# Kernel: gated linear attention and a mixture of experts. The first six units' steps in a written-out order, k times r made to wait for the port, the gate's weights loaded earlier

## The chip, the cores and the metric

One core of one Trainium2 chip. The metric is the device time of one execution of the program in microseconds, as a median over runs. A core has five engines that run on their own and wait for each other by semaphores: TensorE (PE; its weight loads are shown as PEld), VectorE (DVE), ScalarE (ACT), GpSimd (POOL) and SyncE (SP), which here issues nearly all DMA transfers. Each engine takes its instructions strictly in the order in which they were written.

## The reference

All numbers are float32. First a gated linear attention over 4 batches, 8 heads, 768 tokens and a head size of 48, then a mixture of 8 experts of which each token uses one (3072 tokens of 384 values, hidden size 1024):

```python
f = 1.0 / (1.0 + np.exp(-f_logit))
for t in range(S):
    state = f[:, :, t, :, None] * state + np.einsum('bhd,bhe->bhde', k[:, :, t], v[:, :, t])
    y[:, :, t] = np.einsum('bhd,bhde->bhe', q[:, :, t], state)
x = y.transpose(0, 2, 1, 3).reshape(B * S, H * D)
logits = x @ w_gate
expert_idx = np.argmax(logits, axis=1)
# softmax value of the chosen expert is gate_w
y[rows of e] = np.maximum(x[rows of e] @ w1[e], 0.0) @ w2[e]
out = gate_w[:, None] * y
```

## The kernel before

The attention part is cut into 12 units (`NU`). A unit is a chunk of 128 tokens of two batches with all heads; its q, k and f come as tiles of 128 x 8 x 128 (512 KB each), its v as 384 KB. Units 0 and 1 hold the first chunk of the two pairs of batches, 2 and 3 the second chunk, and so on: each unit needs the state of the unit two before it. A unit goes through these steps, each a small function:

- `load`: SP issues the transfers. q has 4 buffers, k 3, f 2, v 3, so that a load waits until the unit that used the buffer is done with it. Hardware DMA transfers also take turns on eight completion semaphores.
- `steps` and `log` (ACT): exp of -f and ln(1 + that), which is minus the logarithm of the forget gate, in g. `total` (DVE): the running sum of it over the chunk, a scan. `growth` (ACT): r = exp(sum). `decay` (ACT): exp(-sum).
- `by_r`: k times r, on DVE for unit 0 and on POOL for all others. `by_decay` (DVE): q times decay. `ends` and `last_decay` (POOL): small copies of the last column.
- `score` (PE): k times q in two halves, `mask` (DVE): four masked copies out of PSUM, `within` (PE): masked scores times v into `yt`.
- `keys` (PE): k transposed into `kp`, `keep` (ACT): copied to `kn`, `added` (PE): kn times v into `dp`, `update` (DVE, then POOL): the new state, the sum of old state and dp, times the last decay. `before` (PE): q times the old state, added to `yt`.
- `settle` (ACT): yt copied to `ys`. `rows` (PE): ys turned to token rows and multiplied with the gate's weights, into `xp`; the weights lie in a tile of constants, `fpack`. `lay` (ACT): the rows copied to `xr`. `Route` (DVE, mostly small instructions): the chosen expert, the place of each token's row in its expert's region, the gate's value; then POOL scatters the rows to DRAM.

The schedule is written by hand (`manual_schedule`): each engine runs its instructions in the order of the calls. Before, units 0 and 1 and part of 2 and 3 are written out call by call ahead of a loop `for n in range(1, NU + 2)`, and the loop has special cases for n of 1, 2 and 3. In an iteration the loop does the scores, keys and dp of unit n, steps of units n + 1 to n + 3 ahead, and rows and routing of unit n - 2. `warm(24)` and `warm(12)` are matmuls of zeros on `pad` that TensorE runs while it has nothing to do.

The constants come in two parts: `load_first_consts` issues the mask and the identity from ACT's queue, `load_consts` the rest from SP's, after q of unit 3. `load_gate` issues four small transfers of the gate's weights into the same tile as the rest of the constants, behind f of unit 5; they wait until the constants have landed.

In `by_r` a k times r on POOL waits for an instruction on DVE, if one stands in the list `routed`:

```python
if routed:
    tc.add_manual_dep(ins, routed.pop().name, SYNC, reason="the port of both")
```

Before, only the loop puts instructions there (the last of `choose` or of `fill`), so k times r of units 1 to 4 waits for its own operands alone.

After the attention part, experts' weights (`w1t`, `w2t`, 1536 KB each) and the scattered rows are loaded, and two wide matrix products per expert run on TensorE (`widen`, `narrow`). The change leaves this part as it is.

Of the kernel before, what the change touches and what calls it, by code (L numbers as in the profile page):

```python
# [118 lines left out]
def _bc(ap, axis, n):  # L119
    shape = list(ap.shape)  # L120
    shape.insert(axis, n)
    return ap[tuple([slice(None)] * axis + [None])].to_broadcast(shape)
# [3 lines left out]
def kernel(  # L126
# [41 lines left out]
    def load_first_consts():  # L168
        nc.scalar.dma_start(mpack, nc.inline_tensor(mv, name="c_mpack").ap())
        nc.scalar.dma_start(ident, fdram[:, slice(*fat["ident"])])  # L170
# [249 lines left out]

    with ExitStack() as st:
# [25 lines left out]
        routed = []  # L447
        SYNC = mybir.DependencyInfo(mybir.DependencyClass.Sync, mybir.DependencyReason.DATA)
# [8 lines left out]
        def load(u, names, parts=(slice(None),)):  # L457
            x = units[u]
            for n in names:
                src = {"q": qu, "k": ku, "f": fu, "v": vu}[n]  # L460
                if n == "v":
                    x[n] = ld.tile([128, 2, H, D], F32, name=n, bufs=3)
                else:
                    x[n] = held[n][u % len(held[n])]
                for part in parts:
                    nc.sync.dma_start(x[n][:, part], src[u][:, part])
# [19 lines left out]
        def total(u, part=whole):  # L486

            x = units[u]
            if "sum" not in x:
                x["sum"] = wk.tile([128, SEG, CR], F32, name="sum")  # L490
            nc.vector.tensor_tensor_scan(  # L491
                x["sum"][:, part].rearrange("p s c -> p (s c)"),
                x["g"][:, part].rearrange("p s c -> p (s c)"),
                cap[:, part].rearrange("p s c -> p (s c)"),
                0.0,
                OP.add,
                OP.min,
            )
# [25 lines left out]
        def last_decay(u):  # L524
            x = units[u]
            x["last"] = wk.tile([128, SEG], F32, name="last", bufs=3)
            nc.gpsimd.tensor_copy(x["last"], x["dec"][:, :, C - 1])  # L527

        def by_decay(u, part=whole):
            x = units[u]  # L530
            q = x["q"][:, part]
            nc.vector.tensor_tensor(q, q, x["dec"][:, part], op=OP.mult)
# [32 lines left out]
        def within(u, a):  # L565

            x = units[u]
            if a == 0:
                x["yt"] = yt
            for p, h, _ in heads():  # L570
                nc.tensor.matmul(  # L571
                    x["yt"][DP * (h ^ a) : DP * (h ^ a) + D, a, p],
                    lhsT=x["v"][:, a, 2 * p + h],
                    rhs=x["at"][:, a, h, p],
                    start=p == 0,
                    stop=x["old"] is None,
                    skip_group_check=True,
                )
# [38 lines left out]
        def update(u):  # L617

            x = units[u]
            new = wk.tile([128, SEG, D], F32, name="state", bufs=4)  # L620
            last = _bc(x["last"], 2, D)
            if x["old"] is None:
                nc.vector.tensor_copy(new, x["dp"])
            else:
                nc.vector.tensor_tensor(new, x["dp"], x["old"], op=OP.add)
            states[u % 2] = new
            return lambda: nc.gpsimd.tensor_tensor(new, new, last, op=OP.mult)
# [70 lines left out]
        load(0, "f", ab)  # L698
        load(0, "kq")
        load(1, "f")  # L700
        load_first_consts()
        load(1, "kq")
        for i in (1, 0):
            nc.gpsimd.memset(scores[i], 0.0)
        def warm(count):

            for _ in range(count):
                nc.tensor.matmul(yt[:, 0, 0], lhsT=pad[:, 0:C], rhs=pad[:, 0:C], start=True, stop=True)

        warm(24)  # L710
        for part in ab:
            steps(0, part)
            total(0, part)
        load(2, "f")
        load(0, "v")
        for part in ab:
            growth(0, part)
            by_r(0, part, nc.vector)
            decay(0, part)
            by_decay(0, part)  # L720
        ends(0)
        last_decay(0)
        for part in ab:
            steps(1, part)
        load(3, "f")
        load(2, "k")
        load(1, "v")
        load(2, "q")
        load(3, "q")
# [44 lines left out]
        score(0, 0)  # L774
        score(0, 1)
        keys(0)
        warm(12)
        for part in ab:
            total(1, part)
        for a in range(2):  # L780
            for h in range(2):
                mask(0, a, h)
        for part in ab:
            growth(1, part)
            by_r(1, part)
        for part in ab:
            decay(1, part)
            by_decay(1, part)
        ends(1)
        last_decay(1)  # L790
        steps(2)
        total(2)
        keep(0)
        steps(3, logs=False)
        growth(2)
        load_consts()
        load(3, "k")
        load(4, "f")
        load(2, "v")
        load(5, "f")  # L800
        load_gate()

        for n in range(1, NU + 2):
# [3 lines left out]
            rt = None  # L807
            if here < NU:
                units[here]["old"] = states[here % 2]
            if 2 <= last:  # L810
                settle(last)
            if later and later[0] < NU - 1:
                later[1].weigh()
# [3 lines left out]
            if ahead and n != 2:  # L817
                by_r(n + 1)
                ends(n + 1)
# [7 lines left out]
            if n == 1:  # L827
                units[0]["old"] = None
                added(0)
                update(0)()  # L830
            if ahead and not 1 < n < 4:
                decay(n + 1)
                last_decay(n + 1)
# [3 lines left out]
            if n == 2:  # L837
                growth(n + 1)
                by_r(n + 1)
                ends(n + 1)  # L840
            if 1 < n < 4:
                decay(n + 1)
                last_decay(n + 1)
# [4 lines left out]
            if n == 1:  # L848
                log(3)
                within(0, 0)  # L850
                within(0, 1)
                settle(0)
# [6 lines left out]
            if 2 < n < NU - 2:  # L859
                total(n + 2)  # L860
            if n == NU - 2:
                by_decay(n + 1)
            first_half = 1 < n < NU - 2
            if first_half:
                within(back, 0)
            if 0 <= last:
                rt = rows(last, later[1] if later else None)
                lay(last)
# [6 lines left out]
            if n == 2:  # L875
                total(n + 2)
# [13 lines left out]
            if n == 2:  # L890
                settle(1)
            if n + 2 < NU and n != 1:
                growth(n + 2)
# [7 lines left out]
            if n == 1:  # L901
                total(3)
# [15 lines left out]
            if n == 1:  # L918
                load(n + 3, "q")
# [4 lines left out]
            if 1 < n and n + 3 < NU:  # L924
                load(n + 3, "q")
            if n + 5 < NU:
                load(n + 5, "f")
            if n == 1:
                load_first_pads()
# [398 lines left out]
```

## Time and profile before

| | |
|---|---|
| median of 14 runs | 400.96 us (399.82 to 403.68) |
| profiled execution | 400.77 us, span 398.9 us, mean granted TensorE clock 0.983 |
| TensorE busy | 382.2 us of the span (96%) |
| DVE, ACT, POOL busy | 170.3, 103.1, 116.7 us |
| DMA | 95.04 MB, mean 238 GB/s |
| DMA from 5 to 25 us | 383 to 411 GB/s |
| span of the attention part | 0 to about 121 us |

The span is from the first to the last instruction; the profiled execution's own time is 1.9 us longer. Busy times say how long an engine ran, not whether the end waited for it. The timeline merges equal instructions and gives, in brackets, how long the engine was idle before and which instruction released it. Each fp32 matmul of the program appears as two instructions in the trace. Line numbers (L543) are those of the kernel before.

### The profile page before, as it was taken

Reading aid. Unit: us, or ns where it says so; the run is one execution under the profiler, and the core shown is the slowest. Engines: PE = TensorE matmul, PEld = TensorE weight load, DVE = VectorE, ACT = ScalarE, POOL = GpSimd, SP = SyncE. Lnnn points to the kernel's source line nnn. Section 1 sums busy time; section 2 is a strip of 40 time slices with the busy share of each in tenths; the row PEclk is TensorE's granted clock in tenths of the full one; section 3 lists DMA queues with packets and bytes.
Section 4 is the critical chain, followed back from the end, with each engine's and each line's share of the span. In section 5 each row is a group of like instructions: output and inputs, shape, how many; then the busy total and the mean of one; then the engine's idle time right before and its main releaser. Section 6 shows DMA issues by size and latency. Waiting matters only on the chain.

```text
span 398.9 us, 7727 instructions
## 1 busy us (share of the span) xinstructions
PE 382.2 (96%) x3062; PEld 269.1 (67%) x3062; DVE 170.3 (43%) x365; ACT 103.1 (26%) x190; POOL 116.7 (29%) x118
## 2 busy tenths in 40 slices
PE   7898999999997999999999999999999999999993
PEld 7877898999986787777555555664556556555462
DVE  6899988989661452212112113113712113111360
ACT  6888877774431100000010010010000000001000
POOL 5378868797607220010100100100100100100011
PEclk9999999999998699999999999999999999999998
DMA  8999657679954157959339899989145349994141
GB/s 287 391 332 361 235 204 258 231 223 330 399 164 156 50 165 221 306 137 302 103 117 361 228 379 393 282 341 340 39 154 196 99 144 394 397 413 154 26 175 41
DMA packets 51515, 95.04 MB, mean 238 GB/s; under 512 B 20824, under 2 KB 40731, under 8 KB 49424
## 3 DMA queue, kind: packets, MB, share of 16 engines
q1 hardware_dynamic: 48016, 84.76, 62.6%
q0 software_dynamic: 3168, 9.64, 6.4%
q8 instruction: 25, 0.41, 0.4%
q10 hardware_dynamic: 288, 0.08, 0.2%
q14 instruction: 18, 0.15, 0.1%
HBM read 79.46 MB, written 15.21 MB: 237 GB/s over the span
## 4 chain that ended last, share of the span: by engine, by line
PE 86%; DMA 4%; DVE 3%; ACT 2%; issue 1%; another core or an unknown queue 1%; SPq 0%; POOL 0%; POOLq 0%; DVEq 0%; ACTq 0%
PE hps L316 27%; PE yps L332 23%; PE yps L1107 7%; PE xp L663 5%; DMA f<-in_fu_dram 4%; PE yt L571 4%; PE s L543 4%; PE s L316 3%; PE hps L1081 3%; PE yp L332 3%; PE yt L592 3%; PE dp L608 2%; PE kp L558 2%; DVE sum L491 1%
## 5 line engine op out<-in xcount | busy, mean ns | idle before, releaser
L316 PE MATMUL hps<-xT,w1t 128*128 128x352 f32 (+2 forms) x384 | 110.1, 447 | 0.0
L316 PEld LDWEIGHTS hps<-xT,w1t 128*128 128x128 f32 x384 | 72.7, 190 | 37.2 <-issue 1.9
L332 PE MATMUL yps<-w2t,hT 128*128 128x384 f32 x288 | 94.4, 487 | 0.0
L189 POOL DMA_INDIRECT out_dram<-ysb,dst x24 | 23.3, 969 | 224.5 <-DVE ysb L343 216.1
L332 PEld LDWEIGHTS yps<-w2t,hT 128*128 128x128 f32 x288 | 54.6, 190 | 38.6 <-issue 1.5
L326 ACT ACTIVATE hT<-hps 128x352 f32<-128x352 f32 (+2 forms) x28 | 13.7, 491 | 200.7 <-PE hps L316 190.6
L328 DVE TENSOR_SCALAR hT<-hps 128x352 f32<-128x352 f32 (+2 forms) x28 | 15.6, 558 | 93.0 <-PE hps L316 93.0
L343 DVE TENSOR_SCALAR ysb<-yps,tg 128x384 f32<-128x384 f32 x22 | 13.6, 618 | 74.4 <-PE yps L332 55.7
L189 POOL DMA_INDIRECT xs<-xr,posi x24 | 33.1, 1381 | 25.4 <-DVE ex L222 12.7
L549 DVE COPY_PREDICATED at<-mpack,s 128x512 f32<-128x512 uint8 x48 | 31.1, 730 | 6.2 <-PE s L543 6.2
L509 POOL TENSOR_TENSOR k<-k,r 128x1024 f32<-128x1024 f32 (+1 forms) x12 | 26.5, 2213 | 19.9 <-ACT r L505 10.5
L491 DVE TENSOR_TENSOR_SCAN sum<-g,cap 128x1032 f32<-128x1032 f32 (+1 forms) x14 | 28.9, 2061 | 3.1 <-ACT g L484 3.0
L663 PE MATMUL xp<-fpack,ys 128*128 128x104 f32 x192 | 26.0, 285 | 2.1 <-ACT ys L633 1.4
L1107 PE MATMUL yps<-qw,hqT 128*32 128x192 f32 (+1 forms) x192 | 26.9, 381 | 0.0
L543 PE MATMUL s<-q,k 64*128 64x128 f32 x384 | 24.7, 278 | 2.0 <-POOL last L527 1.4
L663 PEld LDWEIGHTS xp<-fpack,ys 128*128 128x128 f32 x192 | 23.2, 194 | 4.4 <-issue 1.8
L571 PE MATMUL yt<-at,v 128*48 128x128 f32 x384 | 25.1, 277 | 0.0
L543 PEld LDWEIGHTS s<-q,k 64*128 64x128 f32 x384 | 22.4, 188 | 3.9 <-POOL last L527 1.6
L571 PEld LDWEIGHTS yt<-at,v 128*48 128x48 f32 x384 | 20.0, 123 | 2.6 <-issue 1.5
L1107 PE MATMUL yps<-w2t,hT 128*32 128x384 f32 x192 | 21.4, 487 | 0.0
L316 PE MATMUL s<-xT,w1t 128*128 128x128 f32 x96 | 15.5, 316 | 2.0 <-issue 1.9
L633 ACT COPY ys<-yt 128x512 f32<-128x512 f32 x24 | 12.9, 592 | 16.2 <-PE yt L592 11.6
(114 smaller groups left out, 366.3 us busy)
## 6 DMA issues: line engine op xcount, KB each, us to landing
qw<-in_moe_w_dram SPq DMA_DIRECT2D x16, 1536.0 KB
w1t<-in_moe_w_dram SPq DMA_DIRECT2D x8, 1536.0 KB
w2t<-in_moe_w_dram SPq DMA_DIRECT2D x8, 1536.0 KB
k<-in_ku_dram SPq DMA_DIRECT2D x12, 512.0 KB
q<-in_qu_dram SPq DMA_DIRECT2D x12, 512.0 KB
f<-in_fu_dram SPq DMA_DIRECT2D x11, 512.0 KB
xs<-pad SPq DMA_DIRECT2D x8, 600.0 KB
v<-in_vu_dram SPq DMA_DIRECT2D x12, 384.0 KB
```

Source lines behind the costliest of these rows:

```text
L189: ins = nc.gpsimd.indirect_dma_start(out=dst, out_offset=bass.IndirectOffsetOnAxis(ap=idx, axis=0), in_=src, in_offset=None, bounds_check= ...
L316: nc.tensor.matmul(x["h"][:, f], lhsT=w[0][:, j, b * 128 : b * 128 + 128], rhs=x["xT"][:, j], start=j == 0, stop=j == KD - 1,)
L326: nc.scalar.activation(to, x["h"], AF.Relu)
L328: nc.vector.tensor_scalar(to, x["h"], 0.0, None, op0=OP.max)
L332: nc.tensor.matmul(yp, lhsT=x["hT"][:, f, t * C : t * C + C], rhs=w[1][:, f, :], start=f == 0, stop=f == NF - 1,)
L491: nc.vector.tensor_tensor_scan(x["sum"][:, part].rearrange("p s c -> p (s c)"), x["g"][:, part].rearrange("p s c -> p (s c)"), cap[:, part ...
L509: ins = on.tensor_tensor(k, k, units[u]["r"][:, part], op=OP.mult).ins
L543: nc.tensor.matmul(ps[h][:, p], lhsT=x["k"][r, s], rhs=x["q"][r, s], start=True, stop=True)
L549: nc.vector.copy_predicated(x["at"][:, a, h], _bc(causal, 1, HP), x["ps", a][h])
L571: nc.tensor.matmul(x["yt"][DP * (h ^ a) : DP * (h ^ a) + D, a, p], lhsT=x["v"][:, a, 2 * p + h], rhs=x["at"][:, a, h, p], start=p == 0, st ...
L663: nc.tensor.matmul(xp[:, p], lhsT=x["ys"][:, a, p], rhs=wx[:, p, 0:XW] if a else wx[:, p, E:WX], start=True, stop=True,)
L1107: nc.tensor.matmul(yp[r], lhsT=h[:, f, at : at + T], rhs=w[:, f, cols], start=f == 0, stop=f == NF - 1, skip_group_check=True,)
```

## The change

The calls ahead of the loop and the loop's iterations 1 to 5 give way to a table, `FIRST_STEPS`. Each word is a piece of work, a unit and sometimes a half; a loop over the table calls the piece. The loop proper now starts at n = 6. The sets of transfers and of computing steps stay; their order on each engine changes:

- PE: 17 and 4 zero matmuls instead of 24 and 12; the keys of a unit ahead of its scores; in units 1, 2, 4 and 5 the two halves of the scores apart; `within` of units 0 and 1 much earlier (that of unit 0 before the keys of unit 1).
- DVE, ACT and POOL: the masks of a unit, the copies, scans and exponentials stand in a new order through unit 8.
- SP: the first constants, which ACT issued, are issued by SP in front of q of unit 0. The other constants stand behind q of unit 2, and the gate's four transfers right behind them, in front of f of unit 4, k of unit 3, v of unit 2 and q of unit 3.
- k times r on POOL in units 1 to 6 waits for the DVE scan or q times decay that was written last before it (`port["latest"]`).
- `last` has four buffers instead of three.

```diff
 def load_first_consts():
-    nc.scalar.dma_start(mpack, ...)
-    nc.scalar.dma_start(ident, ...)
+    nc.sync.dma_start(mpack, ...)
+    nc.sync.dma_start(ident, ...)
...
+    FIRST_STEPS = """
+        lf0a lk0 consts0 lq0 lf1 lk1 lq1 fill17 exp0a ln0a scan0a exp0b lf2 lv0 ln0b r0a
+        scan0b dec0a r0b dec0b exp1a byr0a ln1a byd0a byr0b byd0b scan1a exp1b lf3 lk2 lv1
+        lq2 consts1 gate0 kp0 ln1b r1a scan1b sc0a keep0 mask0a r1b sc0b dec1a mask0b byr1a
+        byr1b dp0 fill4 ends0 exp2 lf4 lk3 lv2 lq3 upd0 byd1a wi0a wi0b ln2 kp1 sc1a dec1b
+        keep1 set0 scan2 last1 dp1 last0 ends1 byd1b r2 exp3 lf5 dec2 sc1b lq4 lk4 lv3 ln3
+        mask1a wi1a mask1b byr2 upd1 wi1b byd2 kp2 sc2b scan3 keep2 xp0 ends3 mask2b exp4
+        lf6 pads0 upd0p r3 byr3 lay0 sc2a lk5 lv4 lq5 ends2 dp2 set1 mask2a ln4 wi2b dec3
+        last2 upd2 scan4 wi2a kp3 keep3 bef2 dec4 last3 byd3 byd4 r4 xp1 sc3a exp5 lf7 byr4
+        lay1 upd1p ends4 set2 ln5 sc3b lk6 lv5 lq6 oh1 dp3 mask3a mask3b exp6 lf8 sc4a upd3
+        ln6 last4 kp4 scan5 mask4a wi3a ends5 keep4 r5 wi3b dec5 scan6 wgh1 xp2 bef3 lay2
+        sc4b lk7 lv6 lq7 set3 dec6 place1 exp7 lf9 upd2p dp4 ln7 wi4a mask4b wi4b upd4 byr5
+        byd5 kp5 upd3p scan7 byd6 keep5 bef4 last6 last5 exp8 lf10 xp3 oh3 sc5a mask5a r6
+        sc5b lk8 lv7 lq8 ends6 lay3 dp5 byr6 wgh3 mask5b ln8 r7 set4 upd5 upd4p send5
+    """
...
+    def do_by_r(u, part):
+        routed[:] = [port["latest"]] if u else []
+        by_r(u, piece(part), nc.gpsimd if u else nc.vector)
...
+    for what, u, part in re.findall(r"([a-z]+)(\d+)([abp]?)", FIRST_STEPS):
+        DO[what](int(u), part)
...
-    for n in range(1, NU + 2):
+    for n in range(FIRST, NU + 2):
```

In the table, l stands for a load (lf4: f of unit 4), sc for `score`, kp for `keys`, wi for `within`, dp for `added`, bef for `before`, xp for `rows`, oh, place and wgh for the routing, fill for the zero matmuls.

## The prediction

> **What bounds the kernel now.** I read the page first, then TensorE's timeline of the first 46 us, the busy times by stage, the waits before 42.2 us, and the order of the built instructions, which shows what the table moves.
>
> From the page:
>
> ```profile
> PE 382.2 (96%) x3062; PEld 269.1 (67%) x3062; DVE 170.3 (43%) x365; ACT 103.1 (26%) x190; POOL 116.7 (29%) x118
> PE 86%; DMA 4%; DVE 3%; ACT 2%; issue 1%; another core or an unknown queue 1%; SPq 0%; POOL 0%; POOLq 0%; DVEq 0%; ACTq 0%
> ```
>
> TensorE is the bound, and the 4% of DMA stands at the front. Busy times by stage (stretch and length, then busy us of PE, PEld, DVE, ACT, POOL; granted clock; DMA share; GB/s):
>
> ```profile
> 0.00:42.18 42.18, 35.70 (x457) 32.89 (x457) 36.66 (x47) 34.74 (x59) 27.35 (x27) 1.00 0.91 334
> 42.18:114.00 71.82, 71.82 (x1214) 65.27 (x1216) 59.85 (x139) 47.77 (x88) 51.88 (x50) 1.00 0.79 274
> 126.00:136.00 10.00, 8.00 (x32) 6.72 (x31) 1.75 (x11) 1.62 (x5) 4.66 (x9) 0.50 0.27 105
> ```
>
> From 42.18 to 114 us TensorE has no idle time at all: there the change can bring nothing, and whatever the front saves arrives whole at 114 us and, if the later steps are merely shifted, at the end. So the question is how much TensorE loses before 42.18. Its timeline (start, us, then idle before in brackets):
>
> ```profile
> 9.64 2.06 PE L543 MATMUL s<-q,k 64*128 64x128 f32 x32
> 11.62 1.09 PE L558 MATMUL kp<-fpack,k 128*128 128x128 f32 x8
> 12.55 2.84 PE L708 MATMUL yt<-pad 128*128 128x128 f32 x24
> 16.81 2.06 PE L543 MATMUL s<-q,k 64*128 64x128 f32 x32 [1.42 <-POOL last L527]
> ...
> 24.62 2.06 PE L543 MATMUL s<-q,k 64*128 64x128 f32 x32 [0.57 <-POOL rend L515]
> ...
> 29.07 2.00 PE L663 MATMUL xp<-fpack,ys 128*128 128x104 f32 x16 [0.35 <-ACT kn L563]
> ...
> 33.51 1.14 PE L608 MATMUL dp<-v,kn 128*64 128x48 f32 x32 [1.43 <-ACT xr L693]
> ...
> 42.18 1.14 PE L608 MATMUL dp<-v,kn 128*64 128x48 f32 x32 [0.54 <-ACT xr L693]
> ```
>
> After unit 0's scores and transposed keys (12.55), TensorE loses 2.84 of filler and 1.42 + 0.57 + 0.35 + 1.43 + 0.54 of idle: 7.15 us. This is all that reordering can win after 12.55. What else the front waits for:
>
> ```profile
> POOL k L509 <- ACT r L505: 10.5, 4, 4.4
> ACT g L476 <- DMA f<-in_fu_dram: 3.6, 3, 1.8
> ```
>
> **The sum of the new order.** I walk TensorE's new sequence with the old rows' durations; per unit s 1.99, kp 1.02, dp 0.92, yt of a unit's own chunk 1.9, yt from the state 1.02, xp 1.96; DVE's scan 2.31, four masks 2.57, q times decay 1.28; ACT 0.53 for half a tile, 0.96 for a whole one; k times r on POOL 2.37.
>
> Start. The constants leave ACT's queue and stand on SP's ahead of q of unit 0. ACT's two issues (0.4 each) lay beside its table load of 1.28, and SP's two more are hidden, since the queue's transfers of 1.3 each run behind its issues of 0.45: nothing either way. The first filler, 17 for 24, ends near 8, before the first k is ready. The bytes ahead of unit 1's f are the same, and ACT's start on unit 1 (9.62, released by f) stays. k·r of unit 0 ends at 9.71 on DVE; kp's second half 0.5 and s 1.99 end at 12.2 instead of 12.55. That is lost again, because dp comes next and needs v of unit 0.
>
> v of unit 0. Ahead of its end stand seven tiles of 512 KB, 384 KB of v and 80 KB of constants, 4.14 MB. The DMA moved 0.88 MB by 5 us and 2.01 more by 10; the other 1.25 at 396 GB/s end at 13.2. For f of unit 1 the same count gives 8.2, and ACT was released at 9.6, 1.4 later; so v is there at about 14.5. From 12.55: 1.95 idle. The filler of 4 costs 4/12 of 2.84, 0.95.
>
> Unit 1. yt of unit 0 starts at 16.3 (masks end 13.55 + 2.57 = 16.1, covered). kp, s, dp, s of unit 1 follow unbroken until 22.3. The last two masks then end about 23.5 where TensorE wants them at 23.2: 0.3.
>
> Unit 2. ACT does kn, ys and r from 19.0 and is done at 22.2; k·r on POOL ends at 24.55, and q times decay on DVE at 25.8: TensorE waits 0.1 and 0.2.
>
> The gate's weights. SP meets them right behind the constants they overwrite, and holds f of unit 4, k of 3, v of 2 and q of 3 behind that wait. The constants land at about 21.9 (before they landed one 1.3 us tile later, by 23.2, where SP's wait of 3.4 us for them ended). Four issues take 1.79 and f's own 0.4: 24.2. The first half tile of f took 2.7 from issue to ACT's start, a whole tile 0.65 more: f at 27.5, k at 28.8, v at 29.8, q at 31.1, since the queue has run empty in between. Before, ACT started on that f at 25.86. Then exp 1.15, r 0.96, three copies 0.8 and ys 1.06 end at 31.5; yt of unit 2 wants that at 30.95. k has 0.9 to spare (k·r starts at 29.7), q 3.6, v nothing. TensorE waits 0.25 for dp and 0.55 for yt. Bounds: nothing if f lands a microsecond sooner, 2 us if it and v are 1.2 later, as tails in this trace can be (8.2 against 9.6); I take 0.8.
>
> Units 3 to 5. kp of 4 waits 0.3 for DVE's state; yt of 4 waits 1.0, since its second pair of masks stands behind the scan of unit 6 and the nine small routing steps (0.22 each); s of 5 waits 0.3 and dp of 5 0.3.
>
> The port wait. k·r of unit 5 waits for the scan of unit 6, to 47.9 though r is ready at 45.4. It ends at 50.3, and its transposes come at 53: covered by 2.7; without that cover up to 2.4. Where both engines meet today, POOL already stands still: its copies of 128x8 take 0.19 alone and 2.2 beside a scan. A gain is bounded by what DVE loses to POOL, a scan of 2.62 for 2.31, 0.3 a unit. I take nothing. The behind-queue of each k·r (end copies, state times decay, scatters) has unit-long slack. The fourth buffer of last has no instruction.
>
> Lost after 12.55: 1.95 + 0.95 + 0.3 + 0.3 + 0.8 + 0.3 + 1.0 + 0.3 + 0.3 = 6.2. The same walk through the old order loses 8.0 where the trace shows 7.15, so it overstates waits; scaled by 0.89 the new order loses 5.5. Gain 7.15 - 5.5 = 1.6.
>
> **Rivals.** First, slower: the clock. There are 1.95 to 2.3 us of idle before dp of unit 0, with 4 fillers instead of 12. Against it: 1.42 and 1.43 us of idle left the clock at 1.00. For it: at 125.8 it fell to half for 10.2 us, and in the 3.4 us before TensorE's longest gap was 1.22, its idle time 1.6 in all. If one gap of about 2 us does that, the next 10.2 us, holding 9 us of work, lose up to 5.1, of which the waits of units 1 and 2 and of the gate absorb 1.4 to 2: 3.1 net, 402.3. It decides where more than about half of some 3.4 us is idle.
>
> By the Trainium skill, "TensorE: Matmul & The Clock Gate", Part 1, the clock halves after at least one idle window of about 3.4 us, free-running; a gap of 2.3 would not do, and the sum would stay 399.2. The row at 125.8 fell with less idle than that, so the measurement decides, and I keep this rival.
>
> Second, faster: the late waits aren't there. Of the 6.2, only 1.95, 0.95 and 0.3 for the first masks are forced by rows; the others are small differences between engines that overlap. Without them the loss is 3.2, the gain 3.95: 396.8.
>
> Third, no change: the hole that SP's wait makes costs its upper bound, or v of unit 0 is 1.2 later; the walk then loses as much as the old order: 400.6 and about what it was. For it: the DMA share of 0.91 over the front leaves no reserve.
>
> **How the numbers follow.** The profiled execution took 400.77 (span 398.9 and 1.9 around it), 0.05% under the median of 400.96. 400.77 - 1.6 = 399.2, for which I give 0.4 (its own range 398.2 to 400.0); the clock 0.2 (402.3), the late waits gone 0.2 (396.8), no change 0.2 (400.6). The range from 396.8 to 402.4 takes in the centres of all. About 0.3%, 1.2 us, is what a measurement of this kernel can tell from no change. Faster by more: most of the first case and the second, 0.54; within it: the third and the edges, 0.25; slower: 0.21.
>
> **What would show it.** In the new profile: dp of unit 0 at about 14.5 after 2 us of idle; SP's wait for the constants ending near 22; ACT starting on f of unit 4 near 27.5; the transposed keys of unit 3 near 33.5 (36.56 before, with an equal amount of work behind it); no idle worth a microsecond after 60; the clock at 1.00 until 114. Wrong if the clock dips before 40, if the DMA share in 20 to 26 stays full, or if the stage after 42 shows new waits that add up to the gain.

## The result: 1.4 to 1.8% slower

On the chip of the first comparison the changed kernel takes 407.48 us (median of 10 runs, 403.59 to 409.23), the kernel before 401.38: ratio 1.0136, 95% interval 1.0111 to 1.016. In a later comparison, on a chip where both are faster, it took 397.49 against 390.24: 1.0182, 1.014 to 1.0224. The forecast was 399.2 and a gain. The profiled execution took 409.48 us (span 407.4, clock 0.974).

The page of the changed kernel, the lines that answer to those of before (busy times, and the chain that ended last by engine):

```profile
PE 384.1 (94%) x3032; PEld 268.8 (66%) x3032; DVE 174.6 (43%) x365; ACT 102.6 (25%) x190; POOL 107.1 (26%) x118
PE 84%; DVE 5%; DMA 3%; another core or an unknown queue 3%; ACT 2%; SPq 1%; issue 1%; POOL 0%; POOLq 0%; ACTq 0%
```

TensorE is busy for about as long as before (384.1 us for 382.2) and the span is 8.5 us longer; DVE's share of the chain has gone from 3 to 5%. The busy times by stage say where (columns as before):

```profile
0.00:42.05 42.05, 35.48 (x490) 32.17 (x490) 33.44 (x45) 33.25 (x59) 20.95 (x25) 1.00 0.82 298
42.05:115.00 72.95, 68.92 (x1059) 61.74 (x1060) 63.33 (x128) 47.33 (x84) 48.63 (x52) 0.95 0.74 264
45.00:48.30 3.30, 3.30 (x22) 2.74 (x20) 3.30 (x4) 1.34 (x3) 0.23 (x2) 0.50 1.02 405
```

The stage after 42 us, in which TensorE had no idle time at all, now has 4.0 us of it, and a clock of 0.95: it is at half from 44.94 to 48.35 (third row) and from 68.83 to 72.25. TensorE's waits of more than 0.5 us from 12 to 116 us, from its timeline (two of 0.19 us stand at 24.59 and 57.45):

```profile
14.76 1.14 PE L625 MATMUL dp<-v,kn 128*64 128x48 f32 x32 [2.16 <-ACT r L523]
32.08 1.14 PE L625 MATMUL dp<-v,kn 128*64 128x48 f32 x32 [1.25 <-DMA v<-in_vu_dram]
43.67 1.94 PE L561 MATMUL s<-q,k 64*128 64x128 f32 x16 [1.61 <-DVE at L567]
56.84 0.42 PE L588 MATMUL yt<-at,v 128*48 128x128 f32 x2 [0.55 <-DVE at L567]
67.06 3.82 PE L561 MATMUL s<-q,k 64*128 64x128 f32 x32 [1.48 <-DVE at L567]
```

The last three wait for masks (L567) of units 3, 4 and 5. The front did gain, but half of what was forecast: the keys of unit 3, with about the same work behind them, start at 34.92 instead of 36.56, 1.6 us ahead, where the forecast had 33.5, 3.1 ahead. And at the state's part of y of unit 6, an equal point for both orders, the changed kernel is 6.6 us behind (86.8 against 80.2). The other 1.9 us of the 8.5 come behind that point; in the transition to the experts this profile has one wait of 3.69 us (at 138.1), which the later profile of the same kernel on another chip doesn't have.

Why the masks are late stands in the timeline of POOL and DVE of the changed kernel (some lines left out):

```profile
39.13 2.36 POOL L527 TENSOR_TENSOR k<-k,r 128x1024 f32<-128x1024 f32 x1 [2.81 <-DVE lg L689]
39.26 0.19 DVE L215 TENSOR_REDUCE mx<-lg 128x4 f32<-128x32 f32 x1
39.48 2.06 DVE L216 TENSOR_TENSOR eq<-lg,mx 128x32 f32<-128x32 f32 x1
...
41.45 0.83 POOL L643 TENSOR_TENSOR state<-state,last 128x384 f32<-128x384 f32 x1
...
41.58 0.75 DVE L217 TENSOR_TENSOR eq<-eq,fpack 128x32 f32<-128x32 f32 x1
...
42.80 2.56 DVE L567 COPY_PREDICATED at<-mpack,s 128x512 f32<-128x512 uint8 x4
```

and the same steps in the kernel before (its lines are numbered one lower here):

```profile
37.00 2.37 POOL L509 TENSOR_TENSOR k<-k,r 128x1024 f32<-128x1024 f32 x1 [1.04 <-ACT r L505]
...
43.52 0.19 DVE L215 TENSOR_TENSOR eq<-lg,mx 128x32 f32<-128x32 f32 x1
43.75 0.19 DVE L216 TENSOR_TENSOR eq<-eq,fpack 128x32 f32<-128x32 f32 x1
...
44.72 2.37 POOL L509 TENSOR_TENSOR k<-k,r 128x1024 f32<-128x1024 f32 x1 [1.28 <-DVE ex L222]
```

Two routing steps of 0.19 us each take 2.06 and 0.75. The first ends when k times r of unit 4 ends on POOL (41.49), the second when the product of state and last decay, which stands right behind it there (L643), ends at 42.28. All masks of unit 3 stand behind the two. Before, k times r of unit 4 (37.00) ran ahead of this choice and had no wait, and that of unit 5 (44.72) waited for the end of the choice (`ex`). In the new order each k times r comes one routing step earlier: that of unit 4 beside the choice, that of unit 5 beside the placing, for whose end k times r of unit 6 waited before. And nothing keeps them apart, since the change put the latest scan or q times decay in the place of the old wait. In unit 5 `counts` (L234) takes 1.70 us for 0.17, in unit 6 the two steps take 1.93 and 0.75.

The Trainium skill, "SBUF — State Buffer", section on its two separate sides, says that VectorE and GpSimd share one port pair as an exclusive lock, and that an operation of VectorE with two SBUF inputs (or in a two-port mode) is shut out while a GpSimd operation that reads SBUF holds it. That agrees with the 2.06 us: L216 has two SBUF inputs and ends when k times r does. L215, with one, took its usual 0.19 us beside the same k times r. The copy L234 also has one, from SBUF to SBUF, and was shut out; whether it runs in such a mode no run here shows.

### The profile page after: what moved, and what is told of

It is laid out like the page before. It is cut to its first block, busy times and chain, and to the rows that moved or that the text cites. A ratio compares the mean times of both kernels' runs of the same rounds, so it can differ in the third digit from the quotient of the medians.

```text
span 407.4 us, 7637 instructions
## 1 busy us (share of the span) xinstructions
PE 384.1 (94%) x3032; PEld 268.8 (66%) x3032; DVE 174.6 (43%) x365; ACT 102.6 (25%) x190; POOL 107.1 (26%) x118
## 4 chain that ended last, share of the span: by engine, by line
PE 84%; DVE 5%; DMA 3%; another core or an unknown queue 3%; ACT 2%; SPq 1%; issue 1%; POOL 0%; POOLq 0%; ACTq 0%
PE hps L317 27%; PE yps L333 23%; PE yps L1114 7%; PE yt L588 5%; PE xp L681 5%; PE s L561 3%; PE yp L333 3%; PE hps L1088 3%; PE yt L609 2%; PE kp L576 2%; PE s L317 2%; DMA f<-in_fu_dram 2%; PE dp L625 1%; DMA v<-in_vu_dram 1%; DVE at L567 1%
## 5 line engine op out<-in xcount | busy, mean ns | idle before, releaser
L190 POOL DMA_INDIRECT xs<-xr,posi x24 | 31.9, 1329 | 25.4 <-DVE counts L234 13.4
L567 DVE COPY_PREDICATED at<-mpack,s 128x512 f32<-128x512 uint8 x48 | 31.3, 725 | 5.6 <-PE s L561 5.5
L561 PE MATMUL s<-q,k 64*128 64x128 f32 x384 | 27.8, 287 | 3.3 <-DVE at L567 3.1
L509 DVE TENSOR_TENSOR_SCAN sum<-g,cap 128x1032 f32<-128x1032 f32 (+1 forms) x14 | 27.9, 1992 | 2.9 <-ACT g L502 2.6
L561 PEld LDWEIGHTS s<-q,k 64*128 64x128 f32 x384 | 24.2, 193 | 6.0 <-issue 4.7
L317 PE MATMUL s<-xT,w1t 128*128 128x128 f32 x96 | 14.0, 291 | 2.7 <-issue 2.6
L1114 PEld LDWEIGHTS yps<-w2t,hT 128*32 128x32 f32 x192 | 7.6, 110 | 13.0 <-issue 12.5
```

Of the source, the lines that this page charges most:

```text
L190: ins = nc.gpsimd.indirect_dma_start(out=dst, out_offset=bass.IndirectOffsetOnAxis(ap=idx, axis=0), in_=src, in_offset=None, bounds_check= ...
L317: nc.tensor.matmul(x["h"][:, f], lhsT=w[0][:, j, b * 128 : b * 128 + 128], rhs=x["xT"][:, j], start=j == 0, stop=j == KD - 1,)
L509: port["latest"] = nc.vector.tensor_tensor_scan(x["sum"][:, part].rearrange("p s c -> p (s c)"), x["g"][:, part].rearrange("p s c -> p (s ...
L561: nc.tensor.matmul(ps[h][:, p], lhsT=x["k"][r, s], rhs=x["q"][r, s], start=True, stop=True)
L567: nc.vector.copy_predicated(x["at"][:, a, h], _bc(causal, 1, HP), x["ps", a][h])
L1114: nc.tensor.matmul(yp[r], lhsT=h[:, f, at : at + T], rhs=w[:, f, cols], start=f == 0, stop=f == NF - 1, skip_group_check=True,)
```

## Experiments

Each ratio is against the kernel before in the same comparison on the same chip (389.95 to 390.24 us in all but the last two runs).

**The changed kernel again.**

> The changed kernel itself once more, beside the four below on one chip, where the kernel before took 390.07 us in the first four runs. On the chip of the first comparison the ratio was 1.0136 and its profile had two spells of half clock of 3.41 us that the kernel before lacked. Theory (collisions of k times r with the routing, 1.61 + .55 + .19 + 1.48 us of idle TensorE, and the two spells that follow them, about 3.4 us together): some 6.5 us over the kernel before here too, ratio 1.015 to 1.019. Rival (the loss is in the transition after 140 us, whose wait was 2 us longer in that one profile): ratio about 1.011, without the spells near 45 and 69.

397.49 us, ratio 1.0182 (1.014 to 1.0224). Its trace has the waits of 2.12, 1.61, 1.41 and 1.48 us again and two spells of half clock, one at 16.6, behind the first gap, and one at 67.8. There is no wait in the transition after 126 us on this chip (TensorE 25.93 of 26 us busy), so that was not the cause.

**The routing behind the masks.** `oh1`, `place1` and `oh3`/`wgh3` are moved in the table so that no masks stand behind them.

```diff
-lq6 oh1 dp3 mask3a mask3b exp6 lf8 sc4a upd3 ln6
+lq6 dp3 mask3a mask3b exp6 lf8 sc4a upd3 oh1 ln6
-dec6 place1 exp7 lf9 upd2p dp4 ln7 wi4a mask4b wi4b
+dec6 exp7 lf9 upd2p dp4 ln7 wi4a mask4b place1 wi4b
-xp3 oh3 sc5a ... byr6 wgh3 mask5b ln8 r7 set4 upd5 upd4p
+xp3 sc5a ... byr6 mask5b ln8 r7 set4 upd5 oh3 wgh3 upd4p
```

> The changed kernel with three words of its table moved: the choices of units 1 and 3 (oh1, oh3) and the placing of unit 1 (place1) stand on DVE behind the masks that they stood in front of; nothing else is touched. Theory A (collision): in the changed kernel k times r runs on POOL beside DVE's small two-input steps of the routing, which then take 2.06 and 0.75 us instead of 0.19 each, and the masks and scores behind them come late; this costs the two idle stretches of 1.6 and 1.5 us and the two 3.4 us spells of half clock that follow them. It expects unit 4's keys at 43 (45.5 in the changed kernel), unit 6's at 64.5 (70.8), no half clock between 40 and 75, and 401 to 403 us instead of 407.5. Theory B (the gate's place on SP alone is what costs): same as the changed kernel within 1 us. Theory C (the table's order as such, many small waits): keys of unit 6 not earlier than 69.

394.53 us, ratio 1.0108 (1.007 to 1.0146). The three waits for masks (1.61, 0.74 and 1.48 us) are gone, and in their stretch TensorE waits 0.29, 0.59 and 0.38 us for other things; the keys of unit 6 start at 63.8 instead of 70.8. But a new wait of 1.98 us comes before the state product of unit 6, followed by 6.83 us at half clock. It is the same kind of meeting, one step on:

```profile
65.19 2.39 POOL L527 TENSOR_TENSOR k<-k,r 128x1024 f32<-128x1024 f32 x1
...
66.03 4.63 DVE L509 TENSOR_TENSOR_SCAN sum<-g,cap 128x1032 f32<-128x1032 f32 x1
...
71.31 1.16 PE L625 MATMUL dp<-v,kn 128*64 128x48 f32 x32 [1.98 <-ACT xr L711]
```

A scan of 2.30 us takes 4.63 beside k times r of unit 7 (to 67.58) and the product of the state behind it on POOL (67.65 to 68.49). The gate's sums stand behind the scan and start at 70.59 us, and what waits for them holds TensorE.

**The gate's weights behind q of unit 3**, instead of ahead of f of unit 4: `gate0` moved behind `lq3` in the table.

> The changed kernel with one word of its table moved: the gate's four transfers stand behind f of unit 4, k of 3, v of 2 and q of 3 on SP instead of in front of them. Theory B (hole in the queue): the DMA share in 20 to 25 us, 0.12 in the changed kernel, is about full, dp of unit 2 no longer waits 1.25 us for v, unit 3's keys come at 33.5 to 34 (34.9), and the whole is 1 to 1.5 us faster if this reaches the end. Theory A (collision decides): the front is earlier, but the collision of k times r of unit 4 with the routing stays, so that about 1 us or less is left at the end: 406.5 to 407.5.

395.96 us, ratio 1.015 (1.0133 to 1.0167). The wait of 1.25 us before the state product of unit 2 is gone; half clock at 14.86 and 45.58 us is mixed into the time, so the gate's place was priced again without it (below).

**The old order with the gate's weights early.** In the kernel before, `load_consts()` and `load_gate()` are moved up, behind q of unit 2 and in front of q of unit 3.

> The kernel before with one step of the change alone: the larger part of the constants and the gate's transfers are issued behind q of unit 2, in front of q of 3, k of 3, f of 4 and v of 2. Theory B: SP holds these loads behind its wait for the constants; f of unit 4 comes some 3 us later than before (ACT took it at 25.9), unit 3's keys at 39 to 41 instead of 36.6, and the whole takes 403 to 405. Theory A: the old order has slack there; at most 1 us slower than before.

397.2 us, ratio 1.0176 (1.015 to 1.0201). The loads stand behind the queue's wait (DMA share 0.09 from 20 to 25 us): TensorE stands idle for 6.29 us at 28.65, and half clock follows for 6.83 us. In the old order this part of the change alone, with the half clock that it sets off, costs as much as the whole change, more than either theory gave it.

**The old order with the new wait.** In the kernel before, k times r from unit 5 on waits for the latest scan or q times decay.

```diff
+if u > 4:
+    routed[:] = [port["latest"]]
```

> The kernel before with one step of the change alone, carried through all later units: from unit 5 on, k times r on POOL waits for the DVE scan or q times decay written last before it, and no longer for the last step of the choice or of the placing. Theory A (collision): k times r of 2.4 us runs beside the routing's small steps on DVE, one or two of which take some 2 us instead of 0.19 in every unit from 5 to 11; DVE has about 1 us to spare per unit, so TensorE is no longer without idle time from 42 to 114; 5 to 10 us slower than before. Theory C: no such stretching, within 1 us of before.

394.75 us, ratio 1.0123 (1.0106 to 1.014), with no spell of half clock before 389 us. One routing step in each unit takes about 2 us beside k times r (the first two lines have it for unit 5), VectorE is busy 69.8 of the 72 us from 42 to 114, and TensorE waits in every unit (last line: what waited for what, us in all, times, longest):

```profile
43.31 2.36 POOL L510 TENSOR_TENSOR k<-k,r 128x1024 f32<-128x1024 f32 x1 [0.18 <-ACT r L506]
43.44 2.28 DVE L216 TENSOR_TENSOR eq<-eq,fpack 128x32 f32<-128x32 f32 x1
...
PE dp L611 <- ACT xr L696: 2.9, 7, 0.6
```

So trading the old wait for the new one costs over 1% by itself, in the old order too.

**The old wait in the new order.** k times r of units 4 to 6 waits for the choice or placing before it again (`byr4` behind `oh1`, `port["latest"]` also set by the routing).

> The changed kernel with one rule of the kernel before: k times r of units 4 to 6 waits for the last step of the routing's choice or placing before it (k times r of unit 4 stands behind the choice in program order), not for the latest scan or q times decay. Theory (the lost wait lets k times r run beside the choice, 2.06 us for a step of .19): L216 and L217 take .19 us each, the masks of units 3 and 5 start 2.4 us earlier, the gaps of 1.61 and 1.48 us and the two spells behind them go, and the time falls by 4 to 6.5 us, to within 2 us of the kernel before. Rival (the order itself, not the wait, makes the collision): k times r only meets the next short steps or the masks, gaps of 1 us or more stay at other places, and the time falls by under 2 us.

395.79 us, ratio 1.0126 (1.0102 to 1.0151): 1.7 us less than the changed kernel, where 4 to 6.5 was expected.

```profile
40.23 0.19 DVE L216 TENSOR_TENSOR eq<-lg,mx 128x32 f32<-128x32 f32 x1
...
41.43 2.37 POOL L527 TENSOR_TENSOR k<-k,r 128x1024 f32<-128x1024 f32 x1 [1.60 <-PE s L561]
...
43.85 1.16 PE L561 MATMUL s<-q,k 64*128 64x128 f32 x16 [1.39 <-POOL k L527]
```

The routing takes 0.19 a step again, but k times r of unit 4 starts 1.7 us later (41.43 for 39.77 in the changed kernel on the same chip), and TensorE, which now has its masks in time, waits 1.39 us for k times r instead. It waits 0.95 us for that of unit 6 as well, and 1.53 and 1.96 us before the state products of units 5 and 6. The theory was right on the cause and wrong on the cure: the new order has no room for k times r behind the choice.

**No port wait at all** in the table (`routed[:] = []`).

> The changed kernel with k times r in the written-out order waiting for no scan and no q times decay (the wait that the change added is gone, the collisions of units 4 and 6 with the choice may stay). Theory (the added wait costs little, it was the old wait for the routing that was worth something): within 1.5 us of the changed kernel, 397.49 us on the chip of its last run. Rival 1 (the added wait keeps k times r off the scans and is worth its place): 2 us or more slower, with scans that take over 4 us. Rival 2 (the added wait itself puts k times r onto the choice): 2 us or more faster, L216 back to .19 us.

397.07 us, ratio 1.018 (1.0138 to 1.0221), the changed kernel's time within 0.4 us, where the interval is 1.6 us to either side. L216 still takes 1.69 us. A scan does run beside k times r now, and here it is POOL that loses:

```profile
51.34 2.29 DVE L509 TENSOR_TENSOR_SCAN sum<-g,cap 128x1032 f32<-128x1032 f32 x1
...
51.43 4.35 POOL L527 TENSOR_TENSOR k<-k,r 128x1024 f32<-128x1024 f32 x1
```

The wait that the change added is worth nothing that this can tell; the one it displaced was worth over 1% in the old order.

**Filler in the gaps**: the changed kernel with zero matmuls behind the state products of units 3 and 5.

> The changed kernel with filler products (zeros, nobody reads them) put into the two idle gaps of TensorE at 42.0 and 65.6 us: seven behind the state product of unit 3 and six, added onto a bank as zeros, behind that of unit 5. Each waits for nothing; the gaps' waits themselves stay. Theory A (the half clock is set off by the gaps): both spells of 3.41 us are gone, and the time falls by 3.0 to 3.5 us under the changed kernel. Theory B (the spells come for another cause, as those after 120 us seem to): they stay, and the time is within 0.5 us of the changed kernel. Theory C (filler is not free): up to 1 us slower.

394.86 us, ratio 1.0123 (1.0106 to 1.014), clock 1.00 with no spell before 392 us: 2.6 us less than the changed kernel, somewhat under the 3.0 to 3.5 of theory A. The waits themselves are unchanged (L216 2.06 us), so this is the price of the half clock. Not all of it belongs to the two gaps filled: in the profile of the changed kernel on this chip one of the two spells stood behind the first gap, which is left open here (1.92 us) and happened to pass at full clock.

**All repairs together**: routing behind the masks, gate behind q of unit 3, nine fillers before the first state product, eight before that of unit 6.

> The routing behind the masks (as in the run of that name), the gate's weights behind q of unit 3 (as in the run of that name), nine filler products in front of the first state product (the gap of 2.16 us at 12.6) and eight zeros added in front of the state product of unit 6 (the gap of 1.98 us at 69.3). Theory (gaps set off the half clock; without them the new order is ahead): no spell of half clock before 120 us; the earlier run with the routing moved, 394.53, less 3.4 us of the spell, less about 1 us of the two waits behind the gate: 389 to 391 us, level with the kernel before at 390.07 or a little under it. Rival (the spells come anyway, or the vector engine is what is late): 393 to 395.

391.01 us, ratio 1.0019 (1.001 to 1.0029). No spell; 0.8 us over the kernel before, though it was expected to be level or under it. From here the gate's place and the collisions are put back one at a time, with filler in most of the large gaps, on one chip:

> The version with the routing behind the masks, the gate behind q of unit 3 and both fillers once more, as the footing for the runs beside it: 391.01 us and ratio 1.0019 in its first run; the same within .3 us is expected by every theory here.

> The version with the routing behind the masks and both fillers, with the gate's weights back where the change puts them (in front of f of unit 4, k of unit 3). Without spells of half clock, the difference to that version is the price of the gate's place alone. Theory (the hole in the transfers is real and costs what the waits of TensorE at 24 to 33 us show, 1.25 + .2): 0.8 to 1.5 us more, 391.8 to 392.5. Rival (the vector engine has its own wait at 20 to 30 us and hides it): within .4 us of that version, 390.6 to 391.4.

> The changed kernel's own place of the routing (k times r beside the choice), with the gate behind q of unit 3 and filler in every gap of over 1.2 us (nine before the first state product, seven behind that of unit 3, six zeros behind that of unit 5). Without spells, the difference to the version with the routing behind the masks is the price of the collisions alone. Theory (2 x (1.87 + .56) on the vector engine before the masks of units 3 and 5, 1.5 + .5 before those of unit 4, 6.9 us in all, of which the gaps of TensorE, 1.61 + 1.48 + .74 = 3.8, come through): 394 to 395.5. Rival (most of the loss was the half clock): under 392.5.

391.06 (ratio 1.0026), 392.31 (1.0054, 1.0036 to 1.0072) and 393.95 us (1.0096, 1.0081 to 1.0112), the kernel before 390.01. There is no spell of half clock before 388 us in any of the three. So the gate's early place costs 1.25 us (0.8 in the spans of the profiles) and the collisions 2.9, the latter a little under what was expected of them.

**Less work for the vector engine**: q times decay of units 4 to 6 left out, in the repaired order without the eight fillers, and in the kernel before.

> The version with the routing behind the masks, the gate behind q of unit 3 and nine fillers before the first state product, without the eight zeros before the state product of unit 6, and without q times decay of units 4, 5 and 6 (three of 1.2 us on the vector engine; its output is left out of the products). Theory V (behind the collisions the new order is held up by the vector engine, which waits for TensorE at 20 to 30 us, 6.9 us busy of 10 against 9.97 in the kernel before, and is busy 28.8 of 30 us at 40 to 70): with 3.6 us of its work gone the wait before the state product of unit 6 (1.98 us in the run with the routing moved alone) goes without filler, no half clock follows, and the time is 387.5 to 389.5. Theory T (TensorE's own work is the limit there): 390.5 to 391.5, the same as with the filler, or 393 to 395 if the wait stays and sets off a half clock.

> The kernel before without q times decay of units 4, 5 and 6. Theory V: its TensorE is busy without a gap from 42 us on, so the same 3.6 us of vector work gone give nothing: ratio .998 to 1.002. Theory T's counterpart (the vector engine bounds both orders alike): the same fall as in the run above, 1.5 us or more.

390.2 (ratio 1.0012, 1.0 to 1.0025) and 389.99 us (1.0005, 0.9995 to 1.0015). The old order gains nothing, as expected. In the new one the wait before the state product of unit 6 is down to 0.20 us, without the eight fillers and with no spell, but the time is only level with the kernel before, 0.7 us or more over what theory V gave it. And it doesn't tell a full vector engine from a meeting on the port: with less to do, k times r of unit 7 ran at 63.28, ahead of the scan, which took 2.37 us.

**The scan of unit 8 behind the row sums**, with three fillers and with none.

> The version with the routing behind the masks, the gate behind q of unit 3 and nine fillers before the first state product, with the scan of unit 8 put behind the routing rows of unit 4 on the vector engine, so that the gate's sums (lg) no longer wait behind its 4.6 us, and three zeros left before the state product of unit 6. Theory V says that the vector engine's total is what is late: the state product of unit 6 starts up to 2 us earlier, but the scan ends some 2.5 us later, and a wait of about a microsecond comes later; 390 to 392. Theory O (only the place of the scan is at fault): no gap over .5 us up to 110 us, and 388.5 to 389.5, under the kernel before by .2 to .4%.

> The run with the scan of unit 8 behind the routing rows, without its three zeros before the state product of unit 6. Theory (the new order's waits and filler now cost what those of the old order do): 390.0 to 391.2, level with the kernel before within .3%. Rival (the filler was all that stood in its way): 389.0 or less.

391.13 us (1.003, 1.0021 to 1.004) and 391.9 us (1.0049, 1.0033 to 1.0066). The scan is back to 2.30 us and the wait of unit 6 gone, but waits of 0.6 to 0.8 us come back behind it.

**k times r of unit 7 ahead of the scan, with all work in**: two scatters that stood in front of it on POOL are put behind it.

> The version with the routing behind the masks, the gate behind q of unit 3 and nine fillers before the first state product, without the eight zeros; and the two scatters that stand ahead of k times r of unit 7 on POOL (62.5 to 64.97 us in the run of that version) put behind it, in front of the scatters of the next step. In that version k times r of unit 7 runs at 64.97 to 67.36 and the scan of unit 8 takes 4.63 us beside it, 2.30 elsewhere; the row sums behind it come 2.3 us late, and the state product of unit 6 with them (the wait of 1.98 us, or the filler in its place). Theory C (this third meeting on the port is what is left of the loss): k times r of unit 7 starts near 63.4, the scan takes 2.3 to 2.7 us, the wait before the state product of unit 6 is under .4 us, no half clock; 388.8 to 390.2. Theory V (the vector engine's total, not the meeting): the wait stays above 1 us or returns one unit later; 390.8 or more.

> The same, with the two scatters put one unit later still, behind k times r of unit 8 (in the run above, four scatters of about 1.1 us stand between k times r of units 7 and 8). If k times r of unit 8 is late in the run above (after 73.9 us), this one is faster by up to 1 us; if not, the two are equal within .3 us. Theory C: 388.8 to 390.2; theory V: 390.8 or more.

On a chip where the kernel before took 401.72 us: 405.67 (1.0106, 1.0083 to 1.0128) and 404.71 (1.009, 1.006 to 1.0121), both slower. In the first one:

```profile
63.48 2.39 POOL L527 TENSOR_TENSOR k<-k,r 128x1024 f32<-128x1024 f32 x1 [1.32 <-PE s L561]
...
65.65 2.38 DVE L509 TENSOR_TENSOR_SCAN sum<-g,cap 128x1032 f32<-128x1032 f32 x1
...
75.12 2.36 POOL L527 TENSOR_TENSOR k<-k,r 128x1024 f32<-128x1024 f32 x1
...
76.01 4.56 DVE L509 TENSOR_TENSOR_SCAN sum<-g,cap 128x1032 f32<-128x1032 f32 x1
```

The meeting of unit 7 is gone and with it the wait (the keys of unit 7 start at 72.8 instead of 75.2). One unit later k times r of unit 8 meets the scan of unit 9 in the same way, with a wait of 1.99 us and 3.41 us of half clock. In the second run the later scan takes 3.54 us, the wait is 0.81, and half clock follows as well. So the meeting explains the wait, and taking one away moves it on. In the first run the edit itself has a share in that: the two scatters now stand ahead of k times r of unit 8, which starts at 75.12 for 73.69 in the version with filler. No version here beat the kernel before.

## Where the prediction was right and wrong

The whole difference, in steps of the medians (each on its chip, with the kernel before at 389.95 to 390.24 on all of them):

| step | us | |
|---|---|---|
| half clock | 397.49 to 394.86 | 2.6 |
| gate's place, first gap filled (1.25 when tried by itself) | 394.86 to 393.95 | 0.9 |
| k times r beside the routing | 393.95 to 391.06 | 2.9 |
| what the repaired order still loses | 391.06 to 390.01 | 1.05 |

**Right in part.** The first state product came at 14.76 after 2.16 us (forecast about 14.5 after 1.95); the masks of unit 1 cost 0.19 (0.3). The gate's hole is there: between 20 and 25 us the DMA share is 0.12, 29 GB/s, where it was 1.02 and 411 GB/s. The added port wait itself is worth nothing that the run without it can tell. The prediction had named the place of its own failure, new waits in the stage after 42 that add up to the gain; they add up to more, 3.8 us, with half clock at 44.94 and 68.83 where it expected 1.00 until 114. The front came out 1.4 us short of the forecast (keys of unit 3 at 34.92 for 33.5): 0.45 of it is the gate's, 0.2 the first state product's, and the rest was not divided further.

**The gate, mis-sized.** The four issues took 3.07 us, not 1.79, so f of unit 4 came later (SP's issues and ACT's start on that f, from the timeline of the changed kernel; the bracket names DVE, but the last part of f landed at 29.03 us, just before ACT's start):

```profile
22.11 3.07 SPq L181 DMA_DIRECT2D fpack<-in_moe_w_gate_dram  x4
...
25.28 0.39 SPq L484 DMA_DIRECT2D f<-in_fu_dram  x1
...
29.11 1.06 ACT L494 ACTIVATE g<-f 128x1024 f32<-128x1024 f32 x1 [1.75 <-DVE lg L689]
```

29.11 where 27.5 was forecast, and v of unit 2 cost the state product 1.25 us where 0.25 was forecast; y of unit 2 waited for nothing (0.55). In sum 1.25 us of waiting for 0.8.

**Wrong: "The port wait ... I take nothing".** This is the step that failed. The price of the added wait was right, but the step left out what k times r would now run beside. For units 5 and 6 the same line of the diff discards the old wait, `routed` with the routing's last step. For unit 4, which never had it, the table puts k times r beside a choice ahead of which it had ended by 3.9 us (39.37 against 43.31). In the walk the nine routing steps had "0.22 each", taken from a trace in which k times r stayed off them; in the changed kernel two steps of a unit took 2.06 + 0.75, 1.70 + 0.73 and 1.93 + 0.75, and these meetings cost 2.9 us by themselves, before any half clock. "A gain is bounded by what DVE loses to POOL, a scan of 2.62 for 2.31" looked only at meetings that the old order has. Of the waits forecast for units 4 and 5, the 1.0 for the masks in y of unit 4 is there (0.55 + 0.19). The other three (0.3 each) are in no row; in their place stand 1.61 and 1.48.

**Wrong in place and weight: the clock.** As a rival it had 0.2 and was tied to the gap before the first state product. In the first trace that gap left the clock at 1.00, and half clock followed the two gaps from the collisions; in other runs with the same front it followed the first gap. It was a part of the outcome and not an alternative to the forecast. And "more than about half" of 3.4 us idle was set too high: 1.0 to 1.6 us were enough in some cases (below).

**Wrong: the gain of 1.6 itself.** The repaired order with the third meeting avoided (390.2, less vector work) is no faster than the old one with the same work left out (389.99). Two terms were off, 2.0 us together; that they are the whole reason is a sum and not the result of a run. Scores whose halves stand apart cost TensorE time: all scores take it 19.3 us from 8 to 86 in the repaired order, against 18.5 in the old one, 0.8 that the sum took at nothing. (In the traces they stand apart in units 1, 2 and 4; the two halves of unit 5 run in one piece.) And of the 7.15 us to be won, 4.31 were idle time on the chip of the profile; on another (the old order with less vector work, whose front is unchanged) the same five gaps are 0.75 + 0.57 + 0.22 + 1.00 + 0.53 = 3.07, so 1.2 us of the prize belonged to that chip or execution. The late waits, forecast at 1.9 in all, were about right in size for this version: in the trace of 390.2 TensorE waits 0.29, 0.58, 0.20 and 0.72 us from 42 to 113 us, 1.8 in all, and the old order has no wait there.

## What to carry to other kernels

When a diff replaces a synchronisation, price the one that goes as well as the one that comes: durations taken from a trace in which the old wait did its work don't hold without it. The same holds for an order that kept two instructions apart without any wait. Before moving a long POOL operation with SBUF operands, list every DVE instruction with two SBUF inputs that can fall beside it, the tiny ones too, and the SBUF copies, and what stands behind them. And add up TensorE's idle time over stretches of 3.4 us: a wait of about a microsecond may be followed by half clock for the next stretch.

## What the runs showed of the hardware

**When the clock falls.** In the 20 traces, the half-clock spells within each trace begin on one grid of 3.413 us and last 3.41, 6.83 or 10.24 us, but for the one at the end of the program, which ends with it. Within a trace the grid can be carried back, and TensorE's idle time (neither matmul nor weight load) be counted in each of its windows that ran at full clock, from 7 to 380 us:

| idle in the window | windows | followed by half clock |
|---|---|---|
| 0.5 to 1.0 us | 47 | 0 |
| 1.0 to 1.63 us | 29 | 9 |
| 1.86 us and more | 8 | 8 |

The kernel before has windows of 1.43 us (no drop) and, in its transition at 122.4, 1.51 (drop), and so stood close to it. The Trainium skill, "TensorE: Matmul & The Clock Gate", Part 1, has a free-running window of 3413 ns, and these spells agree with it; it states that the clock halves after at least one idle window of about 3.4 us. Here windows idle for 1.0 to 1.6 us of their 3.41 were enough in 9 of 29 cases. Why some between 1.0 and 1.63 us fall and others don't is not settled.

**Who loses on the port.** Of k times r and a vector instruction with two SBUF inputs, the one that came second waited for the other's end: scans took 4.63 or 4.56 us behind a k times r and the product of the state that follows it (0.8 us), and k times r 4.35 us behind a scan (2.3 and 2.4 alone). Small instructions pay the same: 2.06 for 0.19. So did two with one SBUF input, a copy of 128x8 (1.70 for 0.17) and the addition of a constant (L259 in the old order with the new wait, 1.90 for 0.17); a reduction (L215) did not.

**Chips.** The kernel before took 401 to 402 us in the first and the last comparison and 390 in the others. About 9 of the 11 us between the spans of two of these profiles lie in the transition to the experts (the old order, and its version with less vector work on a faster chip): from 126 to 152 us TensorE is busy 24.00 of 26 us at a clock of 0.81 in the profile of the kernel before, and 26.00 at 1.00 in the repaired order on one of the faster chips; the first of the experts' wide products (`hps`) starts at 152.8 in the kernel before, and at 142.5 in its version with less vector work there, while the last product of the attention part starts at 118.9 and 117.5. What makes the transition slower there was not tested.
